# Moving a copy to VectorE, filling a wait of TensorE, and starting the clock products from a constant

## The chip, the cores and the metric

The kernel runs on 1 core of one Trainium2 chip. The metric is the device time of one execution in microseconds; lower is better. A time covers some 1.8 us more than the span of the trace, so times are compared with times and spans with spans.

## The reference

Six cross layers over a batch of 16384 rows with 416 features, in bf16:

```python
B, F, D, L = 16384, 26, 16, 6        # Din = F * D = 416
def reference(x0, ws, bs):
    x = x0
    for l in range(L):
        proj = jnp.einsum('bd,de->be', x, ws[l]) + bs[l]
        x = x0 * proj + x
    return x
```

## The kernel before

The batch is cut into 8 groups of 2048 rows, and 48 jobs (group, layer) run in an order that lets independent groups interleave. Features lie on the partitions, as three thirds of 128 and a tail of 32. Only the last job (group 7, layer 5) has its rows on the partitions, so that its result can be stored without a turn (a transpose). It has four "rows" (`kk`) of four column groups (`j`). For each, TensorE makes 3 products of 128 features, one of the 32-feature tail and one that adds the bias; ScalarE copies the sum out of PSUM, the memory that TensorE's products are written to (the text calls such a copy an eviction, and a part of PSUM that holds one result a bank), VectorE multiplies by x0 and adds the residual x5, and a store goes out. The residual comes from the job before with features on the partitions and has to be turned: two thirds by DMA, the last third (and the tail) by TensorE into PSUM, from where two copies bring the third to SBUF, the memory in which the other operands lie.

```python
def keep_busy(n, b):                  # products meant only to keep TensorE's clock up
    while n > 0:
        m = min(n, 4)
        add("pe", lambda h, m=m: h.matmul(
            bank(b, n=m * P).rearrange("p (m c) -> p m c", m=m), ones[:, :],
            ones[:, :].unsqueeze(1).broadcast_to([P, m, P]), start=True, stop=True),
            reads=["ones"], writes=[("ps", b)])
        n -= m
keep_busy(22, 7)
# ... cut: everything up to the last job ...
def turned_out(j, b):                 # the two copies of the turned last third
    t = NT - 1
    dst = x5n[:, j:j + 2, :, t * P:NT * P].rearrange("p j k f -> p (j k) f")
    sp_ = psum_t(b).rearrange("p (a f) -> p a f", f=P)
    kw = dict(reads=[("ps", b), "x5 free"], writes=[("x5n", j, t), ("x5n", j + 1, t)])
    if j:
        add("act", lambda h: h.activation(dst, sp_, ACT_F.Copy), **kw)
    else:
        add("dve", lambda h: h.tensor_copy(dst, sp_), **kw)
# ... cut ...
bks = {0: bka, 1: [b0, b3, b1, a0], 2: [a1, a2, a3, b2], 3: [b0, b3, b1, a0]}
store(LAST - 1, 0, 2)                 # group 6, 0.85 MB each
store(LAST - 1, 2, NJ)
for j in range(NJ):
    nat_full(0, j, bks[0][j], True, (0, 1))
turn_tails(b0)
nat_rows(0, bks[0], False)
turn_last(0, b1)                      # 8 turns on TensorE
turned_out(0, b1)
for j in range(NJ):
    if j == 2:
        turn_last(2, b2)
    nat_full(0, j, bks[0][j], False, (2,))
    nat_out(0, j, bks[0])
turned_out(2, b2)
# ... cut: nat_mul, nat_add, nat_store of row 0, then rows 1 to 3 ...
```

Of the kernel before, what the change touches and what calls it, by code (L numbers as in the profile page):

```python
# [3 lines left out]
P = 128  # L4
CH = 512
T32 = 32

ACT_F = mybir.ActivationFunctionType
ALU = mybir.AluOpType
BF16 = mybir.dt.bfloat16  # L10
# [11 lines left out]
class Program:  # L22
# [12 lines left out]
    def add(self, eng, fn, reads=(), writes=(), lane=None, batch=None, hold=False, release=False):  # L35
        op = Op(eng, fn, lane, batch)
        deps = {}
        if eng == "pool":
            writes = list(writes) + ["pool"]
        for t in reads:  # L40
            w = self.writer.get(t)
            if w is not None:
                deps[id(w)] = (w, True)
        for t in writes:
            w = self.writer.get(t)
            if w is not None:
                deps[id(w)] = (w, True)
            for r in self.readers.get(t, ()):
                if id(r) not in deps:
                    deps[id(r)] = (r, False)  # L50
        for d, raw in deps.values():
            if d.lane is None and d.eng == eng and lane is None and (eng == "pe" or not raw):
                continue
            op.deps.append(d)
        for t in reads:
            self.readers.setdefault(t, []).append(op)
        for t in writes:
            self.writer[t] = op
            self.readers[t] = []
        if eng == "dve":  # L60
            if hold:
                self.flush()
                self.held = op
            else:
                self.queue[eng].append(op)
                if release:
                    self.flush()
        else:
            self.queue[eng].append(op)
        if lane is not None:  # L70
            batches = self.lanes.setdefault(lane, [])
            if not batches or batches[-1][0] != batch:
                batches.append((batch, []))
            batches[-1][1].append(op)
        return op
# [123 lines left out]
def bass_standalone__cross_network_dcn__recsys_kernel(  # L199
# [6 lines left out]
    B, D = x0.shape  # L206
    L = ws.shape[0]
    NT = 3
# [16 lines left out]
    n = 0  # L225
# [8 lines left out]
    w3 = [nc.alloc_sbuf_tensor(f"w3_{l}", [P, D], BF16) for l in range(L)]  # L234
# [4 lines left out]
    ones = nc.alloc_sbuf_tensor("ones", [P, P], BF16)  # L239
# [11 lines left out]
    add = pr.add  # L251
# [16 lines left out]
    def bank(b, p0=0, p1=P, n=CH):  # L268
        return psum[p0:p1, b * CH:b * CH + n]
# [3 lines left out]
    def take(n):  # L273
        got = [(ring[0] + i) % 8 for i in range(n)]
        ring[0] = (ring[0] + n) % 8
        return got
# [46 lines left out]
    def quad(g, l, j):  # L323
        q = (j + turn_of(g, l)) % NJ
        return q, slice(q * T32, (q + 1) * T32)
# [210 lines left out]
    def load_nat(j, k0, k1):  # L536
# [6 lines left out]
        reads=["warm"], writes=["warm"])  # L543
# [23 lines left out]
    def keep_busy(n, b):  # L567


        while n > 0:  # L570
            m = min(n, 4)
            add("pe", lambda h, m=m: h.matmul(
                bank(b, n=m * P).rearrange("p (m c) -> p m c", m=m), ones[:, :],
                ones[:, :].unsqueeze(1).broadcast_to([P, m, P]), start=True, stop=True),
                reads=["ones"], writes=[("ps", b)])
            n -= m

    keep_busy(22, 7)

    def psum_t(b):  # L580
        return psum[:, b * CH:(b + 1) * CH].bitcast(BF16)
# [132 lines left out]
    def store(g, j0, j1):  # L714

        rows = out[g * GC + j0 * CH:g * GC + j1 * CH, :]
        o = ost[:, j0 * KK:j1 * KK, :].rearrange("p (j k) f -> p j k f", k=KK)
        pat = "(j p k) f -> p j k f" if g == 0 else "(j k p) f -> p j k f"
        add("sp", lambda h: h.dma_start(rows.rearrange(pat, j=j1 - j0, k=KK), o),
            reads=[("ost", t, j) for t in range(NT + 1) for j in range(j0, j1)],  # L720
            writes=[("out", g, j0)], lane="out", batch=g)
# [132 lines left out]
    g, l = LAST, L - 1  # L854
# [3 lines left out]
    def xcol(t, j, kk):  # L858
        return src(t, j, j + 1)[:, kk * P:(kk + 1) * P]

    def x3col(j, kk):
        return s3[quad(g, l, j)[1], kk * P:(kk + 1) * P]
# [3 lines left out]
    def nat_full(kk, j, b, first, ts=range(NT)):  # L866
        for t in ts:
            add("pe", lambda h, t=t: h.matmul(  # L868
                bank(b, n=D), xcol(t, j, kk), wm[l][:, t, :], start=(first and t == 0),
                stop=(not first and t == NT - 1)),  # L870
                reads=[stok(t, j), ("wm", l)], writes=[("ps", b)])

    def turn_last(j, b):

        t = NT - 1
        for a in (j, j + 1):
            for kk in range(KK):
                o = ((a - j) * KK + kk) * P
                add("pe", lambda h, a=a, kk=kk, o=o: h.transpose(  # L879
                    psum_t(b)[:, o:o + P], xcol(t, a, kk), ident[:, :]),  # L880
                    reads=[stok(t, a), "ident"], writes=[("ps", b)])

    def turned_out(j, b):
        t = NT - 1
        dst = x5n[:, j:j + 2, :, t * P:NT * P].rearrange("p j k f -> p (j k) f")
        sp_ = psum_t(b).rearrange("p (a f) -> p a f", f=P)
        kw = dict(reads=[("ps", b), "x5 free"], writes=[("x5n", j, t), ("x5n", j + 1, t)])
        if j:
            add("act", lambda h: h.activation(dst, sp_, ACT_F.Copy), **kw)
        else:  # L890
            add("dve", lambda h: h.tensor_copy(dst, sp_), **kw)

    def turn_tails(b):

# [11 lines left out]
                reads=[("ps", b), "x5 free"], writes=[("x5n", a, NT) for a in range(j, j + n)])  # L906
            j += n

    def nat_rows(kk, bks, first=True):
        for j in range(NJ):  # L910
            r, q = quad(g, l, j)
            add("pe", lambda h, j=j, q=q, r=r: h.matmul(  # L912
                bank(bks[j], n=D), x3col(j, kk), w3[l][q, :], start=first, stop=False, tile_position=(r * T32, 0)),
                reads=tok3 + [("w3", l, r)], writes=[("ps", bks[j])])
        for j in range(NJ):
            r, q = quad(g, l, j)
            add("pe", lambda h, j=j, q=q, r=r: h.matmul(
                bank(bks[j], n=D), ones[q, :], brow[q, :], start=False, stop=False, tile_position=(r * T32, 0)),
                reads=["ones", ("brow", r)], writes=[("ps", bks[j])])

    def nat_out(kk, j, bks):
        extra = x0_all(so) + x03_toks(so) if first_use.pop("on", None) else []
        add("act", lambda h: h.activation(on[:, j, kk, :], bank(bks[j], n=D), ACT_F.Copy),  # L923
            reads=[("ps", bks[j])], writes=extra + [("on", j, kk)])

    def nat_mul(kk, j, n=2):
        o, x0v = on[:, j:j + n, kk, :], x0n7[:, j:j + n, kk, :]
        toks = [("on", a, kk) for a in range(j, j + n)]
        add("dve", lambda h: h.tensor_tensor(o, o, x0v, ALU.mult),  # L929
            reads=toks + [("n7", a) for a in range(j, j + n)], writes=toks)  # L930

    def nat_add(kk, j, n=2):
        o, x5v = on[:, j:j + n, kk, :], x5n[:, j:j + n, kk, :]
        toks = [("on", a, kk) for a in range(j, j + n)]
        add("dve", lambda h: h.tensor_tensor(o, o, x5v, ALU.add),  # L935
            reads=toks + [("x5n", a, t) for a in range(j, j + n) for t in range(NT + 1)], writes=toks)
# [9 lines left out]

    a0, a1, a2, a3 = bka = take(NJ)
    b0, b1, b2, b3 = take(NJ)
    bks = {0: bka, 1: [b0, b3, b1, a0], 2: [a1, a2, a3, b2], 3: [b0, b3, b1, a0]}
    store(LAST - 1, 0, 2)  # L950
    store(LAST - 1, 2, NJ)
    for j in range(NJ):
        nat_full(0, j, bks[0][j], True, (0, 1))
    turn_tails(b0)
    nat_rows(0, bks[0], False)
    turn_last(0, b1)
    turned_out(0, b1)
    for j in range(NJ):
        if j == 2:
            turn_last(2, b2)  # L960
        nat_full(0, j, bks[0][j], False, (2,))
        nat_out(0, j, bks[0])
    turned_out(2, b2)
    last = KK - 1
    for j in (0, 2):
        nat_mul(0, j)
# [1 line left out]
        nat_add(0, j)  # L968
    nat_store(0, 0, NJ)
    for kk in range(1, KK):  # L970
        nat_rows(kk, bks[kk])
        for j in range(NJ):
            nat_full(kk, j, bks[kk][j], False)
            nat_out(kk, j, bks[kk])
            if kk == last:
                nat_mul(kk, j, 1)
            elif j % 2:
                nat_mul(kk, j - 1)
                nat_add(kk, j - 1)
            if kk == last and j == 1:  # L980
                nat_add(kk, 0)
                nat_store(kk, 0, 2)
        if kk < last:
            nat_store(kk, 0, NJ)
# [33 lines left out]
```

## Time and profile before

| | kernel before |
|---|---|
| time, median of 3 launches | 475.75 us (475.42 to 475.87) |
| profiled launch | span 476.0 us, time 477.81 us |
| TensorE busy | 470.3 us (99%) |
| VectorE busy | 404.2 us (85%) |
| ScalarE busy | 342.0 us (72%) |

From the page of the kernel before, the busy time of each engine and the shares of the chain that ended last:

```profile
PE 470.3 (99%) x3407; PEld 200.9 (42%) x3407; DVE 404.2 (85%) x699; ACT 342.0 (72%) x372; POOL 6.3 (1%) x15
PE 96%; DMA 2%; ACT 1%; DVE 1%; SPq 0%; issue 0%; DVEq 0%
```

TensorE sets the time nearly everywhere. A change at the edges, outside that long middle, can win only what it takes off the first or last few microseconds.

### The profile page before, as it was taken

How to read it: one execution, taken by the hardware profiler on the slowest of the kernel's cores; microseconds unless marked ns; L12 is line 12 of the kernel's file. 1: busy time of each engine (PE TensorE's matmuls, PEld its weight loads, DVE VectorE, ACT ScalarE, POOL GpSimd, SP SyncE). 2: the span in 40 equal slices, each digit the busy share in tenths (PEclk: the TensorE clock that was granted, in tenths of full speed). 3: DMA queues.
4: the chain of work that ended last, by engine and by line, in shares of the span. 5: the costliest groups of instructions: out<-in, count | busy, mean ns of one | idle time of the engine just before them, and what ended most of it. 6: DMA issues, size and time to landing. Idle time of an engine off the chain costs nothing.

```text
span 476.0 us, 8464 instructions
## 1 busy us (share of the span) xinstructions
PE 470.3 (99%) x3407; PEld 200.9 (42%) x3407; DVE 404.2 (85%) x699; ACT 342.0 (72%) x372; POOL 6.3 (1%) x15
## 2 busy tenths in 40 slices
PE   8999999999999999999999999999999999999996
PEld 4434444654444444444444444444444444444442
DVE  1798888888888888898889869988888888888897
ACT  3677777777777777777777777777777777777776
POOL 1000000000000000000000000000000000001000
PEclk9999999999999999999999999999999999999999
DMA  8986830650001398469409940890001029125899
GB/s 223 171 173 143 185 88 1 110 113 1 19 16 30 65 240 147 67 134 239 111 12 170 240 102 10 175 289 2 1 1 35 0 56 232 34 45 101 222 175 288
DMA packets 138651, 53.18 MB, mean 112 GB/s; under 512 B 112362, under 2 KB 138100, under 8 KB 138612
## 3 DMA queue, kind: packets, MB, share of 16 engines
q1 hardware_dynamic: 138456, 52.54, 49.9%
q8 instruction: 26, 0.43, 0.4%
q14 instruction: 13, 0.11, 0.1%
q10 hardware_dynamic: 156, 0.11, 0.1%
HBM read 5.97 MB, written 13.63 MB: 41 GB/s over the span
## 4 chain that ended last, share of the span: by engine, by line
PE 96%; DMA 2%; ACT 1%; DVE 1%; SPq 0%; issue 0%; DVEq 0%
PE ps L471 78%; PE ps L492 7%; PE ps L513 7%; PE ps L868 1%; PE ps L486 1%; DMA wm<-in_ws_dram 1%; ACT tw L398 1%; PE ps L504 1%; PE ps L592 1%; DMA ot<-x 1%; DVE tw L407 0%; PE ps L879 0%; ACT x L923 0%; DVE x L929 0%; DVE x L935 0%; PE ps L912 0%
## 5 line engine op out<-in xcount | busy, mean ns | idle before, releaser
L398 ACT ACTIVATE tw<-ps,bias 128x1024 bf16<-128x1024 f32 (+1 forms) x295 | 299.8, 1071 | 119.5 <-PE ps L492 81.1
L471 PE MATMUL ps<-x,wm 128*128 128x512 bf16 (+1 forms) x1755 | 380.9, 373 | 0.5 <-DMA wm<-in_ws_dram 0.5
L471 PEld LDWEIGHTS ps<-x,wm 128*128 128x128 bf16 x1755 | 165.3, 98 | 210.0 <-issue 29.3
L407 DVE TENSOR_TENSOR tw<-tw,x 128x1024 bf16<-128x1024 bf16 (+1 forms) x285 | 192.7, 684 | 51.8 <-ACT tw L398 51.2
L412 DVE TENSOR_TENSOR x<-tw,x 128x1024 bf16<-128x1024 bf16 (+1 forms) x285 | 182.6, 681 | 0.0
L492 PE MATMUL ps<-x,w 32*128 32x512 bf16 x512 | 39.2, 379 | 0.0
L513 PE MATMUL ps<-x,wm 128*32 128x512 bf16 x564 | 33.0, 380 | 0.0
L438 ACT ACTIVATE ts<-ps,bias 128x512 bf16<-128x512 f32 x47 | 28.8, 701 | 0.0
L442 DVE TENSOR_TENSOR x<-ts,x 128x512 bf16<-128x512 bf16 x47 | 18.7, 419 | 3.9 <-DMA x<-x 3.8
L513 PEld LDWEIGHTS ps<-x,wm 128*32 128x32 bf16 x564 | 13.8, 96 | 17.6 <-issue 5.3
L492 PEld LDWEIGHTS ps<-x,w 32*128 32x128 bf16 x512 | 7.8, 92 | 26.9 <-issue 26.4
L440 DVE TENSOR_TENSOR ts<-ts,x 128x512 bf16<-128x512 bf16 x47 | 18.6, 419 | 0.0
L602 DVE COPY x<-ps 128x512 bf16<-128x512 bf16 x5 | 2.0, 423 | 10.7 <-PE ps L592 10.7
L712 POOL COPY ost<-ot 128x512 bf16<-128x512 bf16 x6 | 4.8, 805 | 424.3 <-DMA ot<-x 424.3
L868 PE MATMUL ps<-wm,x 128*128 128x416 bf16 x48 | 9.5, 340 | 0.0
L604 ACT ACTIVATE x<-ps 128x512 bf16<-128x512 bf16 x7 | 3.8, 595 | 7.4 <-PE ps L592 7.4
L923 ACT ACTIVATE x<-ps 128x416 bf16<-128x416 f32 x16 | 7.8, 526 | 1.6 <-PE ps L868 1.5
L868 PEld LDWEIGHTS ps<-wm,x 128*128 128x128 bf16 x48 | 4.3, 98 | 4.2 <-issue 1.0
L504 PE MATMUL ps<-x,w 32*32 32x512 bf16 x188 | 5.9, 374 | 0.0
L486 PE MATMUL ps<-x,w 32*32 32x512 bf16 x208 | 5.6, 385 | 0.0
L929 DVE TENSOR_TENSOR x<-x,x 128x832 bf16<-128x832 bf16 (+1 forms) x10 | 4.9, 502 | 0.6 <-ACT x L923 0.4
L935 DVE TENSOR_TENSOR x<-x,x 128x832 bf16<-128x832 bf16 (+1 forms) x9 | 4.7, 540 | 0.2
(41 smaller groups left out, 35.4 us busy)
## 6 DMA issues: line engine op xcount, KB each, us to landing
out_dram<-ost SPq DMA_DIRECT2D x6, 1664.0 KB, 7.0
x<-x SPq DMA_DIRECT2D x24, 96.0 KB, 2.1
wm<-in_ws_dram SPq DMA_DIRECT2D x6, 312.0 KB, 3.4
x<-in_x_dram SPq DMA_DIRECT2D x8, 208.0 KB, 4.8
x<-in_x_dram SPq DMA_DIRECT2D x4, 416.0 KB, 8.3
out_dram<-ost SPq DMA_DIRECT2D x2, 832.0 KB, 5.5
x<-x SPq DMA_DIRECT2D x22, 64.0 KB, 2.0
out_dram<-x SPq DMA_DIRECT2D x3, 416.0 KB, 4.1
```

The costliest lines, as they stand in the source:

```text
L398: add("act", lambda h, a=a, w=w, b0=b0: h.activation(tw[r][:, a * CH:(a + w) * CH], psum[:, b0 * CH:(b0 + w) * CH], ACT_F.Identity, bias=b ...
L407: add("dve", lambda h, a=a, e=e: h.tensor_tensor(tw[r][:, a * CH:e * CH], tw[r][:, a * CH:e * CH], x0s[s0][:, i * GC + a * CH:i * GC + e * ...
L412: add("dve", lambda h, a=a, e=e: h.tensor_tensor(xs[so][:, i * GC + a * CH:i * GC + e * CH], tw[r][:, a * CH:e * CH], src(i, a, e), ALU.ad ...
L438: add("act", lambda h: h.activation(ts[r][:, :], bank(b), ACT_F.Identity, bias=bias[:, 3, l:l + 1], scale=1.0), reads=[("ps", b), "bias"], ...
L440: add("dve", lambda h: h.tensor_tensor(ts[r][:, :], ts[r][:, :], x03, ALU.mult), reads=[("ts", r)] + tok0, writes=[("ts", r)], release=True)
L442: add("dve", lambda h: h.tensor_tensor(x3s[so][:, :], ts[r][:, :], res, ALU.add), reads=[("ts", r)] + rtok, writes=[("x3", so), ("x3", so, ...
L471: add("pe", lambda h, t=t, j=j, k=k, w=w: h.matmul(bank(banks[j])[:, k * w:(k + 1) * w], wm[l][:, t, ecols], src(t, j, j + 1)[:, k * w:(k ...
L486: add("pe", lambda h, q=q, j=j, r=r, c=c, o=o: h.matmul(psum[o, banks[j] * CH:(banks[j] + 1) * CH], w3[l][q, i * P + c * T32:i * P + (c + ...
L492: add("pe", lambda h, q=q, j=j, r=r: h.matmul(bank(banks[j]), w3[l][q, ecols], src[q, :], start=first and not inner, stop=not first and no ...
L504: add("pe", lambda h, l=l, b=b, s3=s3, ri=ri, qi=qi, ro=ro, qo=qo: h.matmul(psum[qo, b * CH:(b + 1) * CH], w3[l][qi, NT * P:D], s3[qi, :], ...
L513: add("pe", lambda h, t=t, j=j, src=src, l=l, b=b, ro=ro, qo=qo: h.matmul(psum[qo, b * CH:(b + 1) * CH], wm[l][:, t, NT * P:D], src(t, j, ...
L868: add("pe", lambda h, t=t: h.matmul(bank(b, n=D), xcol(t, j, kk), wm[l][:, t, :], start=(first and t == 0), stop=(not first and t == NT - 1)),
```

## The change

Three parts. At the end, both copies of the turned last third go to VectorE, which rids ScalarE of a 1.03 us copy ahead of its evictions. Two products of the second row are made early, where TensorE waits for the data that it is to turn; the banks are dealt out anew so that the early bank is free in time. At the start, the products meant to keep the clock up read a constant that exists before the kernel's body begins, and there are 25 blocks of them instead of 22.

```diff
+        one = nc.const_aps.tensor(1.0, [P, CH], BF16)
...
-                bank(b, n=m * P).rearrange("p (m c) -> p m c", m=m), ones[:, :],
-                ones[:, :].unsqueeze(1).broadcast_to([P, m, P]), start=True, stop=True),
-                reads=["ones"], writes=[("ps", b)])
+                bank(b, n=m * P), one[:, 0:P], one[:, 0:m * P], start=True, stop=True), writes=[("ps", b)])
-    keep_busy(22, 7)
+    keep_busy(25, 7)
...
-        if j:
-            add("act", lambda h: h.activation(dst, sp_, ACT_F.Copy), **kw)
-        else:
-            add("dve", lambda h: h.tensor_copy(dst, sp_), **kw)
+        add("dve", lambda h: h.tensor_copy(dst, sp_), **kw)
...
-    bks = {0: bka, 1: [b0, b3, b1, a0], 2: [a1, a2, a3, b2], 3: [b0, b3, b1, a0]}
+    bks = {0: bka, 1: [b0, b1, b2, a0], 2: [a1, a2, a3, b3], 3: [b0, b1, b2, a0]}
...
     nat_rows(0, bks[0], False)
-    turn_last(0, b1)
-    turned_out(0, b1)
+    nat_full(1, 1, bks[1][1], True, (0, 1))
+    turn_last(0, b2)
+    turned_out(0, b2)
     for j in range(NJ):
         if j == 2:
-            turn_last(2, b2)
+            turn_last(2, b3)
+            turned_out(2, b3)
         nat_full(0, j, bks[0][j], False, (2,))
         nat_out(0, j, bks[0])
-    turned_out(2, b2)
...  (row 1 then leaves out the two products already made)
```

More of the change, by code (lines that the diff above doesn't have):

```diff
@@ L907, in turn_tails, with nat_rows @@
             j += n
-    def nat_rows(kk, bks, first=True):
+    def nat_rows(kk, bks, first=True, begun=()):
         for j in range(NJ):
@@ L912, in nat_rows @@
             add("pe", lambda h, j=j, q=q, r=r: h.matmul(
-                bank(bks[j], n=D), x3col(j, kk), w3[l][q, :], start=first, stop=False, tile_position=(r * T32, 0)),
+                bank(bks[j], n=D), x3col(j, kk), w3[l][q, :], start=first and j not in begun, stop=False, tile_position=(r * T32, 0)),
                 reads=tok3 + [("w3", l, r)], writes=[("ps", bks[j])])
@@ L970, in bass_standalone__cross_network_dcn__recsys_kernel @@
     for kk in range(1, KK):
-        nat_rows(kk, bks[kk])
+        begun = (1,) if kk == 1 else ()
+        nat_rows(kk, bks[kk], begun=begun)
         for j in range(NJ):
-            nat_full(kk, j, bks[kk][j], False)
+            nat_full(kk, j, bks[kk][j], False, (2,) if j in begun else range(NT))
             nat_out(kk, j, bks[kk])
```

## The prediction

> **What bounds the kernel now.** I read the page's chain of work that ended last first. It says 96% TensorE: over almost the whole span nothing but matmuls sets the time, and the change touches none of those 450 us. What it touches are the first 6 us and the last 15 us, so I went on with the timeline and the waits of these two stretches. The chain, in order of time, ends like this (start us, us, what):
>
> ```profile
> 466.98 2.21 PE ps L868 x12
> 469.19 0.29 PE ps L912 x4
> 469.48 0.18 PE ps L917 x4
> 469.66 0.65 PE ps L868 x3
> ...
> 470.33 0.52 ACT x L923
> ...
> 471.41 0.39 DVE x L929
> ```
>
> L868 are the products of the last job with the rows on the partitions, L912 and L917 its 32-row part and its bias, L923 the eviction on ScalarE, L929 the product with x0 and L935 the sum on VectorE. TensorE is followed up to two evictions before the end; then VectorE runs back to back from 471.41 to 473.55, and the last store lands near 475.5.
>
> Where TensorE stands still in the tail is in the timeline of its weight loads (start us, us, then the idle time before them and who ended it). L879 turns the last third of the residual, 128 columns at a time:
>
> ```profile
> 461.61 0.23 PEld L879 LDWEIGHTS ps<-ident,x 128*128 128x128 bf16 x4 [0.34 <-DVE x L412]
> 462.08 0.23 PEld L879 LDWEIGHTS ps<-ident,x 128*128 128x128 bf16 x4 [0.25 <-DVE x L412]
> 462.26 0.15 PEld L868 LDWEIGHTS ps<-wm,x 128*128 128x128 bf16 x2
> 462.75 0.56 PEld L879 LDWEIGHTS ps<-ident,x 128*128 128x128 bf16 x8 [0.33 <-DVE x L412]
> ```
>
> Idle weight loads are not idle matmuls, so I worked out the real waits from the matmul starts. A turn follows the one before it by 0.06 us, a product by 0.178. Four turns from 461.61 end at 461.85, and the next starts at 462.08: 0.23 waited. Two products from 462.32 end at 462.67, the next turn starts at 462.75: 0.08. Four turns end at 462.99, the next starts at 463.09: 0.10. Together **0.41 us** in which TensorE waits for L412, the sum that makes the last third. The first idle time (0.34 before 461.61) is not such a wait: a product comes 0.28 us after the first bias matmul in the later rows too, where nothing is waited for.
>
> The same stretch on ScalarE and VectorE, from their timelines:
>
> ```profile
> 462.95 0.68 DVE L891 COPY x<-ps 128x1024 bf16<-128x1024 bf16 x1
> 463.65 0.59 DVE L929 TENSOR_TENSOR x<-x,x 128x832 bf16<-128x832 bf16 x1
> 464.51 1.03 ACT L889 ACTIVATE x<-ps 128x1024 bf16<-128x1024 bf16 x1
> 464.66 0.59 DVE L929 TENSOR_TENSOR x<-x,x 128x832 bf16<-128x832 bf16 x1 [0.41 <-ACT x L923]
> 466.39 0.59 DVE L929 TENSOR_TENSOR x<-x,x 128x832 bf16<-128x832 bf16 x1
> 467.02 0.59 DVE L935 TENSOR_TENSOR x<-x,x 128x832 bf16<-128x832 bf16 x1
> ```
>
> L891 and L889 are the two copies of the turned third: one on VectorE, 0.68 us, the other on ScalarE, 1.03 us. The reader is to see that ScalarE's copy stands before the evictions of the second row (they start at 465.41, though their products began at 464.23), and that VectorE still has gaps: it idles before 464.66, and again before 466.39.
>
> At the start:
>
> ```profile
> PE ps L572 <- POOL ones L522: 1.0, 1, 1.0
> PE ps L471 <- DMA wm<-in_ws_dram: 0.5, 1, 0.5
> ```
>
> L572 are the products that only keep TensorE busy; they wait until 0.99 us for a tile of ones. The first real products wait 0.5 us, until 6.46, for the first weights.
>
> [...] the 512-column products at 6.84, 7.27, 7.70 follow each other by 0.43 us, those at 10.99, 11.21, 11.42 by 0.215. [...]
>
> **The change part by part.**
>
> *The copy to VectorE.* Removed from ScalarE: 1 x 1.03 us. Added to VectorE: 1 x 0.68, in effect 0.70 to the next start (462.95 to 463.65).
>
> *Two products early.* Two products of the second row go between the bias matmuls and the first turns: 2 x 0.178 = 0.36 us, into the 0.41 us of waits. They come to start at 461.61; the turns then run 461.99 to 462.47, two products to 462.82, the next turns from 462.84, and those of the last quarter from 463.09 again, as before, for their input is ready only at 463.03. So the second row starts at 463.77 as before but has 10 products instead of 12: **all later matmuls come 0.36 us earlier.** The banks allow it: the order of the evictions L398 frees the early bank first (460.56), the first turned one at 461.14, the second at 461.71, each before its use; and the second row's reuse of the first turned bank waits for the copy that ends at 463.63, before 463.77.
>
> *ScalarE after it.* Rid of the copy, it evicts the second row as the products come: its second eviction ends at about 465.94 instead of 466.36.
>
> *VectorE after it.* I walked its queue with the spacings of the trace: independent operations of 832 columns 0.51, a sum right behind its own product 0.63, copies 0.70, the single-width ones 0.29, and 0.40 for a sum right behind. From 462.95: copy, copy, product 464.35, product 464.86 (0.20 later than now), sums 465.36 and 465.87, second row's product at 466.38 (now 466.39), 467.01, 467.52, 468.14; third row 468.65, 469.28, 469.78, 470.40; last row 470.91, 471.20, then the sum at **471.60 instead of 471.81**. At each step I checked ScalarE's eviction against it: the evictions are always done (last row's second at 471.02). So from the first copy on VectorE never waits, and it becomes the bound of the tail. As a sum: its present waits are 0.50 (464.16 to 464.66), 0.21 (466.18 to 466.39), 0.08 and 0.13, together 0.92; less the added 0.70 leaves 0.22. **The tail gains 0.21 us, not the 0.36 that TensorE gains.**
>
> *The constant for clock products.* The wait for the tile of ones goes: the products can start at about 0.72, right after the barrier that the other engines leave at 0.73, 0.27 us earlier. They are now 25 blocks of 0.107 = 2.67 us, ending at 3.39, where the first turns start today (3.38, on a load). Nothing on the chain moves: the first weights still land at 6.3, with 0.5 us of slack. Direct gain 0.
>
> Sum: 475.75 - 0.21 = 475.54.
>
> **The rivals.** (a) *TensorE's gain comes through whole*, 0.36 us: 475.4. For it: the chain names TensorE until 470.31. Against: the walk above; VectorE has 2.27 us of work a row against TensorE's 2.68, so it could win back 0.4 us a row, but it starts 0.20 late and only three rows follow. (b) *The stores bind.* From 464.5 to 471.5 the DMA share is at about 1.1 and 335 GB/s, so a store issued earlier could only queue. Against: by the trace's windows the share falls to 0.82 at 471.5 and to 0.69 at 474.0, and the last store lands 1.9 us after its issue, what an idle queue gives small copies too. If it bound, the gain would be 0.1 or less: 475.7. (c) *The clock rises earlier.* In this trace it rises between 10 and 11 us. [...] the first six products (0.215 us less each, 1.3 us) and the 24 turns after them (0.6) would run at full speed, up to 1.9 us: 473.7. For it: that seems to be the intent of three more blocks. [...] (d) *VectorE loses more than I think*, if the second copy waits for its turns: they end at 463.33 plus some 0.2, just before 463.65. A slip of 0.2 would eat the gain: 475.75.
>
> **How the range and the chances follow.** 475.54 less a little for (c) gives 475.5. Three runs of the kernel before lie 0.45 us apart, more than the effect, so the range is mostly theirs: 474.8 to 476.0, with (c) on the low side and (d) on the high side. 2% is 9.5 us; all the work that moves is under 3 us, so "within 2%" is nearly certain.
>
> **What would show it right or wrong.** In the profile after: two products (L867) at 461.6 ahead of the turns, and the waits for L412 down to 0.1 us or less; the distance from second to third row 2.32 us instead of 2.68; two copies back to back on VectorE from about 462.95, and no idle time on VectorE before its products from there to the end; ScalarE idle longer before each row; the last sums about 0.2 us earlier against the start of the copies, while the last matmul is 0.36 earlier. At the start the first product at about 0.7, the first real one still at 6.4 to 6.5. It would be wrong [...] if VectorE idles in the tail, or if the stores' time to landing grows by what was gained.

The sum came to 475.75 - 0.21 = 475.54, and with a little taken off for rival (c) to 475.5. The 0.21 was worked out from the trace alone. How large the little was rested on a rule for when the clock rises that no run here shows. The clock rising earlier, seen as products 0.215 us apart at 7 us, was to count against the prediction. It came: in the profile after they start at 6.43, 6.64 and 6.86, though the clock rises early in most launches of the kernel before as well (below).

## The result, and the profile after

| | before | after |
|---|---|---|
| time, median of 6 launches | 475.81 us (475.40 to 476.77) | 475.62 us (475.46 to 477.69) |
| ratio | | 1.0002, 95% interval 0.9983 to 1.0021 |
| profiled launch | span 476.0, time 477.81 | span 473.9, time 475.70 |

A ratio here and below is the mean time of one kernel's runs over that of the other's of the same rounds, so not quite the ratio of the medians beside it. The two kernels are the same within 2%, and within the noise. The spans differ by 2.1 us, but the times of the two profiled launches do as well, so this is not the change. The chains of the two kernels in the first microseconds show what it is (start us, us, what; "issue" is time in which an engine waits for nothing that the profile shows). Before:

```profile
6.33 0.14 issue
6.46 2.72 PE ps L471 x6
9.18 1.97 PE ps L592 x24
11.16 1.29 PE ps L471 x6
```

After:

```profile
6.08 0.14 issue
6.21 1.46 PE ps L471 x6
7.67 1.34 PE ps L591 x24
9.01 1.32 PE ps L471 x6
```

L471 are the first six real products, L591 and L592 the 24 turns after them. The same six products took 2.72 us in one launch and 1.46 in the other, the turns 1.97 and 1.34: together 1.9 us. Another 0.25 us is that the first weights landed later (the first product at 6.46 against 6.21). In the first launch TensorE still ran at half the rate: its products start 0.43 us apart (6.84, 7.27, 7.70), those of the kernel after 0.215 (6.43, 6.64, 6.86). The turns follow the clock in the same way: 0.107 us each ahead of the rise and 0.056 behind it. The clock record of the trace begins with full speed at 10.4 us there and at 3.5 us in the profile after. So **the profile of the kernel before happens to be one of a late launch**, and its front cannot be set against that of the kernel after. The tails can, if each is measured from a mark of its own.

The clock products do start earlier, as the waits of TensorE after the change show (us in total, times, longest):

```profile
PE ps L573 <- PEq L1001: 0.8, 1, 0.8
PE ps L471 <- DMA wm<-in_ws_dram: 1.0, 1, 1.0
```

The wait for the tile of ones is gone, and the first starts at 0.77 us instead of 0.99. The first real product still waits for the weights, 1.0 us now.

In the tail, the timeline of the weight loads after the change (L867 products, L878 turns; start us, us, idle time before and its releaser):

```profile
459.49 0.11 PEld L867 LDWEIGHTS ps<-wm,x 128*128 128x128 bf16 x2 [0.34 <-ACT tw L398]
459.68 0.61 PEld L878 LDWEIGHTS ps<-ident,x 128*128 128x128 bf16 x8
460.24 0.15 PEld L867 LDWEIGHTS ps<-wm,x 128*128 128x128 bf16 x2
460.71 0.56 PEld L878 LDWEIGHTS ps<-ident,x 128*128 128x128 bf16 x8 [0.32 <-DVE x L412]
```

The two products stand ahead of the turns, and the first eight turns run without a wait between them. VectorE after the change:

```profile
460.91 1.28 DVE L887 COPY x<-ps 128x1024 bf16<-128x1024 bf16 x2
462.11 1.10 DVE L925 TENSOR_TENSOR x<-x,x 128x832 bf16<-128x832 bf16 x2
463.13 1.08 DVE L931 TENSOR_TENSOR x<-x,x 128x832 bf16<-128x832 bf16 x2
...
468.64 0.75 DVE L925 TENSOR_TENSOR x<-x,x 128x416 bf16<-128x416 bf16 x2
```

Both copies run back to back, and what follows has no idle time before it but a little at 468.64, where two 0.37 us products take 0.75 because the second (469.01) waits for its eviction (until 468.98). From the start of the first copy (460.91; 462.95 before) to the end of the last sum it now takes 10.25 us, against 10.59: the engines finish **0.34 us sooner**. Yet the last store lands 12.50 us after that copy, against 12.58. The windows of the last microseconds name what took the rest (columns: window and length; PE, PEld, DVE, ACT, POOL busy us and count; TensorE clock; DMA share; GB/s). Before, around the last sum at 473.55:

```profile
472.50:473.00 0.50, 0.00 (x0) 0.00 (x0) 0.50 (x3) 0.00 (x0) 0.00 (x0) 1.00 1.08 348
473.00:473.50 0.50, 0.00 (x0) 0.00 (x0) 0.50 (x2) 0.00 (x0) 0.00 (x0) 1.00 0.86 263
473.50:474.00 0.50, 0.00 (x0) 0.00 (x0) 0.05 (x1) 0.00 (x0) 0.00 (x0) 1.00 0.99 336
474.00:474.50 0.50, 0.00 (x0) 0.00 (x0) 0.00 (x0) 0.00 (x0) 0.00 (x0) 1.00 0.69 225
```

After, around the last sum at 471.16:

```profile
470.00:470.50 0.50, 0.00 (x0) 0.00 (x0) 0.50 (x3) 0.04 (x1) 0.00 (x0) 1.00 1.08 333
470.50:471.00 0.50, 0.00 (x0) 0.00 (x0) 0.50 (x3) 0.00 (x0) 0.00 (x0) 1.00 1.11 338
471.00:471.50 0.50, 0.00 (x0) 0.00 (x0) 0.16 (x1) 0.00 (x0) 0.00 (x0) 1.00 1.06 325
471.50:472.00 0.50, 0.00 (x0) 0.00 (x0) 0.00 (x0) 0.00 (x0) 0.00 (x0) 1.00 0.81 246
```

Before, the DMA share dips to 0.86 while the last stores are issued; after, it stays at 1.06 or more until the last one is out (issued at 473.58 before and 471.19 after). Behind the last issue it falls in both (0.69 and 0.81). Time from issue to landing over the six stores of group 7 (min, median, max), before and then after:

```profile
DMA to landing us min/median/max: 1.9/2.8/5.3
```

```profile
DMA to landing us min/median/max: 2.2/3.0/5.2
```

The shortest times are those of the last two, small stores; that of the very last is 0.3 us more (1.94 and 2.22). What the engines won, the last store seems to wait in a full queue. One profile of each is thin evidence, so this became the theory to test.

### The profile page after: what moved, and what is told of

Its sections match the earlier page's. It is cut to its first block, busy times and chain, and to the rows that moved or that the text cites. A ratio compares the mean times of both kernels' runs of the same rounds, so it can differ in the third digit from the quotient of the medians. Undisturbed runs are those within 1.5% of the kernel's fastest.

```text
span 473.9 us, 8467 instructions
## 1 busy us (share of the span) xinstructions
PE 467.7 (99%) x3408; PEld 199.5 (42%) x3408; DVE 404.5 (85%) x700; ACT 340.9 (72%) x371; POOL 6.0 (1%) x15
## 4 chain that ended last, share of the span: by engine, by line
PE 94%; DMA 2%; DVE 2%; ACT 1%; SPq 0%; issue 0%; DVEq 0%
PE ps L471 78%; PE ps L492 7%; PE ps L513 7%; PE ps L486 1%; DMA wm<-in_ws_dram 1%; DVE x L931 1%; DVE x L925 1%; DMA x<-x 1%; ACT tw L398 1%; PE ps L504 1%; DMA ot<-x 1%; PE ps L591 0%; DVE tw L407 0%; SPq L537 0%; ACT ost L709 0%
## 5 line engine op out<-in xcount | busy, mean ns | idle before, releaser
L471 PE MATMUL ps<-x,wm 128*128 128x512 bf16 (+1 forms) x1755 | 379.6, 372 | 1.0 <-DMA wm<-in_ws_dram 1.0
L471 PEld LDWEIGHTS ps<-x,wm 128*128 128x128 bf16 x1755 | 165.1, 98 | 209.7 <-issue 28.2
L867 PE MATMUL ps<-wm,x 128*128 128x416 bf16 x48 | 9.7, 340 | 0.0
L867 PEld LDWEIGHTS ps<-wm,x 128*128 128x128 bf16 x48 | 4.2, 98 | 4.4 <-issue 1.0
```

The source lines that it names most:

```text
L471: add("pe", lambda h, t=t, j=j, k=k, w=w: h.matmul(bank(banks[j])[:, k * w:(k + 1) * w], wm[l][:, t, ecols], src(t, j, j + 1)[:, k * w:(k ...
L867: add("pe", lambda h, t=t: h.matmul(bank(b, n=D), xcol(t, j, kk), wm[l][:, t, :], start=(first and t == 0), stop=(not first and t == NT - 1)),
```

## The experiments

**Theory S**: the queue of stores binds the end; the change moves the engines out of its way and wins nothing. **Rival V**: only engines bind, and the gain at the end (0.2 to 0.35 us) is real but hidden in the noise of the times. **Theory of the groups of launches**: they are made by when TensorE's clock rises, not by the kernel.

The table collects the tail of all profiles. All columns are us, counted from the start of the first copy on VectorE, which itself does not move (it starts 0.67 us after the pair of sums ahead of it in both kernels, 462.28 to 462.95 and 460.24 to 460.91): last sum of VectorE done; last landing of a store; and for the store that is issued last, issue to landing. In all runs but e12 that store is also the last to land. These columns come from one profiled launch a row. The last two columns are the median time and the ratio to the kernel before of the same rounds.

| run | last sum | landed | issue to landing | time | ratio (95%) |
|---|---|---|---|---|---|
| before, first profile | 10.59 | 12.58 | 1.94 | 475.81 | |
| after, first profile | 10.25 | 12.50 | 2.22 | 475.62 | 1.0002 (0.9983 to 1.0021) |
| e1 before again | 10.59 | 12.49 | 1.86 | 475.58 | 0.9992 (0.9975 to 1.0010) |
| e2 after again | 10.24 | 12.50 | 2.22 | 475.47 | 0.9993 (0.9974 to 1.0012) |
| e3 before, one store less | 10.60 | 12.39 | 1.76 | 476.26 | 1.0004 (0.9986 to 1.0021) |
| e4 after, one store less | 10.25 | **12.04** | 1.76 | 475.59 | 0.9999 (0.9977 to 1.0020) |
| e5 end of the change only | 10.24 | 12.55 | 2.27 | 475.93 | 0.9994 (0.9974 to 1.0015) |
| e6 copy only | 10.59 | 12.54 | 1.91 | 475.64 | 0.9988 (0.9964 to 1.0012) |
| e7 early products only | 10.39 | 12.53 | 2.11 | 475.79 | 0.9994 (0.9973 to 1.0015) |
| e8 constant only | 10.61 | 12.52 | 1.88 | 476.02 | 0.9995 (0.9975 to 1.0016) |
| e9 after, store put forward | 12.13 | 13.93 | 1.77 | 476.95 | 1.0024 (1.0011 to 1.0037) |
| e10 after, no clock products | 10.24 | 12.53 | 2.25 | 476.69 | 1.0017 (1.0003 to 1.0031) |
| e11 e9, and weights alone first | 11.86 | 13.65 | 1.76 | 477.67 | 1.0039 (1.0026 to 1.0053) |
| e12 after, 0.85 MB more | 10.25 | **15.23** | 4.75 | 478.26 | 1.0057 (1.0041 to 1.0074) |

### e1 and e2: both kernels again

No edit.

> The kernel before against itself, for the noise, and for a profile of it with the TensorE clock rising early. Theory of the clock: the launches fall into two groups, near 475.5 us and near 477.7 us, by when the clock rises (3.5 us or 10.4 us after the start); expected 475.4 to 476.0 in most launches, a ratio of 1.000, and in an early profile a span of about 474.0 us. If the clock does not make the groups, an early profile is 476.0 us as the first one was.

> The changed kernel again. Theory S (the stores at the end bind): against the first residual copy out of PSUM on VectorE, the last sum ends about 10.25 us later as in the first profile (10.6 before), but the last store lands about 12.5 us later, no more than 0.1 us sooner than in the kernel before. Theory V (nothing but engines bind): the landing comes 0.3 us sooner too, 12.25 us after that copy, and the first profile was a stray. Time under S: 475.5 to 475.8, ratio 0.9995 to 1.000; under V: 475.4, ratio 0.9993.

The kernel before came out at 0.9992 against itself, the kernel after at 0.9993: the times cannot tell them apart. This profile of the kernel before was of a launch of 475.42 us with a span of 473.6, as expected of an early one. The tails repeat the first profiles within 0.1 us: 10.59 and 10.24 for the engines, 12.49 and 12.50 for the landing. In windows of 0.5 us the DMA share repeats too: a dip to 0.85 ahead of the last issue in e1, none below 1.07 in e2. The landing follows S, not V.

### e3 and e4: one store less, in both kernels

```diff
-    store(LAST - 1, 0, 2)
     store(LAST - 1, 2, NJ)
```

Half of group 6 is never written, so the result is wrong; the queue at the end is 0.85 MB shorter.

> The kernel before without the first of the two stores of group 6 (0.83 MB that are never written; the result is wrong on purpose), so the queue at the end is 2.5 us shorter. Theory S: in the kernel before the stores only just bind, so it gains little, 0 to 0.2 us, and the last store lands 1.9 us after its issue. Theory V: 0.

> The changed kernel without the same store (wrong on purpose). Theory S: the gain of the engines comes through: 0.3 us below the light kernel before, the last store lands 1.9 us after its issue instead of 2.2. Theory V: as far below the light kernel before as the changed kernel is below the kernel before, with no change of the time to landing.

With room in the queue, both kernels' last stores land 1.76 us after their issue (1.9 was expected), and the kernel after lands at 12.04 against 12.39: **0.35 us sooner, all of what its engines had won.** In the full kernels the same difference was 0.0 to 0.1. That is S. The landing times of the stores of group 7 are now alike in both light kernels, where the full ones had 1.9/2.8/5.3 and 2.2/3.0/5.2. Before, then after:

```profile
DMA to landing us min/median/max: 1.7/2.4/2.7
```

```profile
DMA to landing us min/median/max: 1.7/2.4/2.7
```

The times do not show it. The pair (476.26 and 475.59) differs by more than the tail explains, and the light kernel before came out above the full one (475.76 in the same rounds), where 0 to 0.2 us below it was expected. The profiled launch of e3 waited until 6.82 us for its first weights, that of e4 until 6.33. Four of e3's five launches took 476.15 to 476.33 us and one 475.72, though its front is the kernel before's, unchanged; only the one was profiled, and why is open. So S rests on the landings in the profiles, two launches of each full kernel and one of each light one, and not on the times.

### e5 to e8: the parts alone

e5 is the change without its first part (the tile of ones and 22 blocks are back). e6 is the kernel before with this edit:

```diff
-        if j:
-            add("act", lambda h: h.activation(dst, sp_, ACT_F.Copy), **kw)
-        else:
-            add("dve", lambda h: h.tensor_copy(dst, sp_), **kw)
+        add("dve", lambda h: h.tensor_copy(dst, sp_), **kw)
...
             turn_last(2, b2)
+            turned_out(2, b2)
         nat_full(0, j, bks[0][j], False, (2,))
         nat_out(0, j, bks[0])
-    turned_out(2, b2)
```

e7 is e5 with the second copy back on ScalarE and in its old place. e8 is the kernel before with only the constant and `keep_busy(25, 7)`.

> Both changes at the end, without the constant at the start. Theory S (stores bind): from the first product with rows on the partitions (its start is +0) the last matmul ends at about +12.3 instead of +12.6, the last sum at +13.95 instead of +14.25, but the last store lands at +16.2 as in the kernel before; time as the kernel before, ratio 1.000. Theory that the start pays: the tail is not the reason of anything, and the launches are late (477.7) as often as those of the kernel before.

> Only the second copy of the turned third moved to VectorE, no early products. TensorE keeps its waits: last matmul at +12.6; VectorE has work in place of its idle time, so the last sum stays at +14.2 to +14.3 and the landing at +16.2. Were ScalarE's copy what held the tail, the last sum would come 0.2 us or more sooner.

> Only the two early products (with the banks of the change), the second copy still on ScalarE. TensorE ends 0.36 us sooner, at +12.25. ScalarE's copy still delays the second row, VectorE then runs without idle time and the last sum comes at +14.05, 0.2 us sooner only. If VectorE and ScalarE did not hold it, it would come at +13.9. The landing stays at +16.2 if the stores bind.

> Only the start: the constant and 25 blocks. First clock product at 0.77 us instead of 0.99, first real product unchanged (6.2 to 6.5, on the weights); the tail as in the kernel before (+14.25, +16.2). Time as the kernel before in the launches with an early clock, 475.4 to 476.0. If the longer stretch raises the clock more surely, no launch of this one is near 477.7.

Counted from the first product, as these expectations were, the last matmul ended at +12.33 (e5), +12.68 (e6), +12.28 (e7) and +12.76 us (e8), and the last sum at +14.00, +14.35, +14.10 and +14.44: each within 0.2 us, and in the order that was expected. In the table's measure, the copy alone wins 0.0, the early products alone 0.2, both together 0.35 us. So the parts need each other. With the copy alone (e6), TensorE is as late as before, and VectorE waits for the third row's first evictions, which wait for TensorE (us in total, times, longest):

```profile
DVE x L926 <- ACT x L920: 0.2, 1, 0.2
```

With the early products alone (e7), TensorE is ahead, but ScalarE's copy still stands before the evictions of the second row:

```profile
462.52 1.03 ACT L889 ACTIVATE x<-ps 128x1024 bf16<-128x1024 bf16 x1
463.42 3.98 ACT L923 ACTIVATE x<-ps 128x416 bf16<-128x416 f32 x8
464.40 0.59 DVE L929 TENSOR_TENSOR x<-x,x 128x832 bf16<-128x832 bf16 x1
```

The second of these evictions ends at 464.37, and the second row's product on VectorE starts behind it at 464.40, some 0.2 us later than VectorE was free for it (its sum before began at 463.68, and in the profile after the next operation started 0.50 behind the same sum, 464.13 after 463.63). The expectation had VectorE without idle time; its last sum came when expected all the same.

None of the four lands sooner than the kernel before (12.52 to 12.55), and no time differs from it. The constant alone (e8) started its products at 0.77 us and left everything else as it was.

### e9 and e11: an attempt to relieve the queue

If the stores bind, one can try to send some of them earlier. In e9 the first store of group 6 goes between the two DMA turns of the residual:

```diff
 def rest_turn(t):
     for j0, j1 in ((0, NJ),) if t == 0 else ((0, 2), (2, NJ)):
         add("sp", lambda h, j0=j0, j1=j1: h.dma_start_transpose(...))
+            if t == 1 and j0 == 0:
+                store(LAST - 1, 0, 2)
```

> The changed kernel with the first of the two stores of group 6 put between the two turns of the last residual instead of behind them, so that it fills idle time of the queue. Theory S: the queue at the end runs out sooner, the last store lands 1.8 to 2.0 us after its issue instead of 2.2, and copy to landing falls from 12.50 to about 12.2 us; time 475.2, ratio 0.9993. If the queue had no idle time to fill, 12.5 as now; if the second turn of the residual comes too late for the sums, the last sum moves past 10.25 us after the copy and nothing is won.

It was 1.2 us slower. The last store did land 1.77 us after its issue, so the end of the queue was free; but the second turn of the residual now came behind the store and took 5.3 us to land, and VectorE stood waiting for it:

```profile
DVE x L933 <- DMA x<-x: 1.9, 1, 1.9
```

There was no idle time in the queue to fill. In the profile after the change the DMA share is 0.97 to 1.11 in every microsecond from 457 to 471, from the turns on, and whatever goes ahead delays something that is needed. The miss was named in the expectation as a way to fail.

e11 adds to this that two small loads stand between the first weights and the second rows at the start (`load_w3` takes the list as a new argument, cut here):

```diff
     load_wm(0, "sp")
+    load_w3(0, "sp", (0, 1))
     for j in range(1, NJ):
         load_nat(j, 0, 2)
         load_nat(j, 2, KK)
-    load_w3(0, "sp")
+    load_w3(0, "sp", (2, 3))
```

> The store put forward as in the run before, and at the start two of the four small loads of the 32-row weights put between the first weights and the second rows, so that the second rows are asked for 0.9 us later and do not share the queue with the first weights. If the weights bind the start and the queue is shared, the first real product comes at 5.5 to 5.9 us instead of 6.2, and the time falls to 474.9; if the second rows come too late for their turns, the gain is lost there; if the weights' landing is latency, no change (475.2 as the run before).

The first real product came at 5.83 us, in the expected range, but in e1 it came at 5.62 without this edit, so nothing is shown. The time that was expected, 474.9, was missed by far: it was 477.67, 0.7 us worse than e9's. Its profiled launch (477.04) was the fastest of its five, and the cause was not traced.

### e10: without the clock products

```diff
-    keep_busy(25, 7)
```

> The changed kernel without the first 25 blocks of clock products (the short stretches later stay). Theory that the clock makes the two groups of launches: [...] nearly all launches are in the late group, 477 to 478 us, ratio 1.003 to 1.005. If the groups have another cause, 475.6 as before.

The direction was right, the size only half: 476.24 to 477.14 us, some 0.9 above the kernel before of the same rounds. The clock rose at 8.1 us, so the six products were partly slow (2.46 us, between the 1.46 and 2.72 shown above):

```profile
6.06 2.46 PE ps L471 x6
```

The time goes with the moment of the rise, and the clock products are worth about 1 us. But they do not settle the moment: with them it came at 3.5 to 6.2 us in all the other profiles, of both kernels and of their variants, and in the first profile at 10.4. Late launches (over 477 us) were 3 of 45 of the kernel before and 1 of 11 of the kernel after (the first profiled launch, 477.81, not counted); two and one more lay between the groups. That the change makes late launches rarer is not shown.

### e12: more in the queue

```diff
     store(LAST - 1, 0, 2)
+    add("sp", lambda h: h.dma_start(spare, x0[0:2 * CH, :].rearrange("(a p) f -> p a f", p=P)), ...)
     store(LAST - 1, 2, NJ)
```

`spare` is the tile of group 6's x0, which nobody reads any more; the added transfer is a load into it, in rows of 832 bytes like those of the stores. The result stays right.

> The changed kernel with a transfer of 0.85 MB that nothing uses (rows of x0 into a free tile) between the two stores of group 6; the result stays right. Theory S: at the 335 GB/s of this stretch the queue at the end is 2.5 us longer, all of it is seen: the engines are as before (last sum 10.25 us after the copy), the last store lands 4.5 to 4.9 us after its issue instead of 2.2, copy to landing 14.8 to 15.2 us instead of 12.5; time 478 us, ratio 1.005. If the landing were only latency: 12.5 to 12.8 us, 475.6.

The engines did not notice (last sum 10.25 us after the copy), and the last landing came 2.73 us later. The store that was issued last took 4.75 us to land, and the one issued before it landed 0.19 us after it. 0.85 MB in 2.73 us is 312 GB/s, near the 325 to 348 of the full windows above. The stores of group 7:

```profile
DMA to landing us min/median/max: 4.8/5.8/8.0
```

What was added before the end is paid for in full. With e4 this settles S from both sides, in the profiles: take 0.85 MB out, and the gain of the engines appears; put 0.85 MB in, and the end moves by just that transfer.

No version here beats both kernels.

## Why the prediction was right or wrong

The time was right: 475.5 predicted, 475.62 measured (475.47 in e2), and the kernels are the same within 2%. That says little for the sum: the launches of one kernel lie further apart than the 0.2 us that it forecast, so no gain at all would have been as right. The ratio (1.0002, 0.9983 to 1.0021) cannot tell the two apart, and by the landings of the profiles the tail gained 0.0 to 0.1 us. The 0.2 us was put together from steps that did not all hold, and that the number came so near is luck.

**TensorE's gain** was right. The two products came where they were expected, and the last matmul ends 8.57 us after the first copy in both profiles of the kernel after, against 8.92 in both of the kernel before: 0.35 us for the 0.36 predicted.

**VectorE as the new bound** was wrong in one term. The second copy was put at 0.70 us, the distance from the old copy to the next product. That distance held a wait: the product needed an eviction that ended at 463.62, just before its start at 463.65. The two copies in fact follow each other by 0.60 us (460.91 to 461.51), and the product follows the second by as much (462.11). Two terms of 0.70 became 0.60, VectorE was 0.2 us ahead of the walk from there on, and in the last row it waits for an eviction again. So the engines gained 0.35 us, not 0.21: rival (a), TensorE's gain coming through whole, was right about the engines.

**The stores hidden** was the step that failed. Rival (b) was dismissed because the share of the DMA engines falls before the end and because the last store took as little as 1.9 us. Both are true of the kernel before, and neither shows a free queue: the same store takes 1.76 us when the queue is shorter (e3), so its 1.94 and 1.86 us already held 0.1 to 0.2 us of waiting. There was no room left for the 0.35 us. The prediction's own test, "the stores' time to landing grows by what was gained", is what came: 1.9 to 2.2. The working had compared the store with smaller copies elsewhere in the trace (those of 32 and 96 KB issued from 86.5 us on, with a DMA share of 0.00 before them, landed in 1.8 and 2.1 us), and had taken gaps of a few tenths in the queue for a free one.

**No direct gain at the start** was right: the first weights land when they land, and in the first profile after the change TensorE waits for them longer (1.0 us). Not in every launch: in e2, where the clock rose only at 5.6 us, the clock products lasted until the first real product at 5.85, and TensorE's waits list none for the weights.

**The clock** was misread. The prediction took the rise between 10 and 11 us in the one profile as what the kernel does, and gave an early rise a small chance and a time of 473.7. In truth most launches of the kernel before are early ones by their times, and 475.75 was already their time; the profile was of a late one, as its 477.81 us beside that median says. The range was not hurt by it. What the trace shows of the clock is the two rates, 0.43 and 0.215 us from product to product; the rule was not shown. The rise came 2.7 us after the first clock product in the first profile after the change and in e1 (0.77 to 3.48, 0.99 to 3.74), and 9.4 us after it in the first profile before (0.99 to 10.38). What sets the moment is open.

One small reading of the kernel was off: only the first of the two early products carries the start flag, not both. The result is correct.

One thing stays open. Without the launches over 476.5 us, the 9 remaining of the kernel after have a mean of 475.53 and the 40 of the kernel before 475.74. That is 0.2 us, from different rounds and chips, where e1 alone shows the kernel before 0.08% under itself. The tails give none of it, and neither e5 nor e8 shows it alone. If it is real, it lies before the tail.

## What to carry to other kernels

When the engines get faster near the end of a kernel, ask how much room the stores have, in microseconds, and set it against the gain: here a queue with small gaps (a DMA share of 0.86 ahead of the last issue) held the last store by 0.1 to 0.2 us already, and moving a store forward cost 1.2 us, because a turn that was needed stood behind it (e9). Take the cost of an operation in a queue from its distance to an independent neighbour, and check that this distance holds no wait. Before reading a profile, compare the time of the profiled launch with the median; if they differ, part of the profile describes another launch.
